# Converting w_out in two halves of one tile, nearer the front of batch 3, in an attention and two-layer kernel on one core

## The chip, the cores and the metric

The kernel runs on one core of one Trainium2 chip. The metric is device time of one execution in microseconds (us). All durations below come from one profiled execution of the kernel before, or from the times of its three runs.

## The reference, cut to what matters

```python
def reference(...):
    attn_out = _attn_ref(q, k, v)                 # 4 batches, 8 heads, 576 positions, masked softmax
    x = attn_out.transpose(0, 2, 1, 3).reshape(2304, 512)
    a = x @ w1;  b = x @ w2                       # 512 -> 1024
    x = (a * b @ w3) @ w_out                      # moe_w_out: 1024 -> 512
    h = x @ w_in                                  # moe2_w_in: 512 -> 2048
    g = h * (1.0 / (1.0 + np.exp(-1.702 * h)))
    return g @ w_out                              # moe2_w_out: 2048 -> 512
```

The weights arrive in 64-bit floats. The change is about the last factor, `moe2_w_out`, called w_out below.

## The kernel before

**Number formats.** Every matmul operand is split into a high and a low part (`split_hi` at L171 on ScalarE, `split_lo` at L177 on VectorE), and each product is three matmuls (`ORDER`: high times low, low times high, high times high). The 64-bit weights come in as tiles `raw` of 128 x 1024 pairs and are made into 32-bit floats by `to_f32`: two passes on ScalarE (L192 writes the tile `x` from `raw`, L193 scales the low words of `raw` in place) and three on VectorE (L194, L195, L196, all on `x`).

**Stages.** The first 466 us hold attention and the first layer, in four batches of 576 rows; batch 3 is the last of them and runs without attention work beside it. A batch is two halves of 288 columns; each half has eight groups m of two products (L354, 12 matmuls each; ScalarE copies the first to `abf` at L377, VectorE multiplies the second into it at L379, and L171 and L177 split the result into `ab`), and then four output groups n (L400, 24 matmuls over the eight `ab`), each copied to `ysb` by ScalarE (L406) and written to DRAM. All these products go through the four buffers of the PSUM pool `mm`.

Then comes the second layer, in three batches of 768 rows, each with eight quads (function `quad`). A quad has seven products of six matmuls (L666; the operands are `yq` and the split first factor `hl`), called its parts, and the adds and gelu of them on VectorE and ScalarE. After the fourth part of quad i and at its end stand the two output groups of quad i - 1 (`o_group`, L712, nine matmuls each, with the split w_out of that quad, `wt`, called w in the trace). The parts go through the four `mm` buffers too: the fifth part of a quad takes the buffer of the first, so it waits for the ScalarE copy of the first (L684, to the tile `c`).

**What is prepared in batch 3.** `weave` merges lists of functions by the marks between 0 and 1 that they carry; it sets the program order, and a scheduler at build time sets the order on each engine from that, each engine then running strictly in its order. Into batch 3 are woven: the split of the second layer's activations (`y_prep`), the first factor's fetch and split (`w_load(0)`, from the DRAM tensor `widram`), and the eight units of w_out (`u_conv`, units 8 to 15, marks 0.14 to 0.84 less one step). A unit is loaded into `raw` (1024 KB; two buffers, one in each of the pools `cv_a` and `cv_b`, unit i + 2 taking the buffer of unit i), converted in the one buffer `x` of `cv_a`, and written to the DRAM tensor `wodram` (L555, 512 KB). The next unit cannot write `x` before that transfer has landed.

**The join.** After batch 3 the pools of batch 3 and `cv_b` are closed, and the pool `p2`, which holds `c`, `u`, `sg` and the odd first factors, is laid over them. So the first `c` (L684) waits for the last readers of all that: the writes of `ysb` and the conversion of the last unit's `raw`. `wt_load(i)` brings one unit back from `wodram` (L643, into the one `raw` buffer of `cv_a`) and splits it into `wt[i]`; `w_load(n)` brings first factor n from `widram` (L617, into the one `x` buffer) and splits it into `hl`. Between the batches of the first layer and quad 0 the program has `wt_load(0)` and `w_load(1)`, and quad i of the first batch begins with `wt_load(i + 1)`.

All DMAs are issued by SyncE (SP), in its program order, on one queue.

Of the kernel before, what the change touches and what calls it, by code (L numbers as in the profile page):

```python
# [11 lines left out]
F32 = mybir.dt.float32  # L12
F32R = mybir.dt.float32r
# [8 lines left out]
P = 128  # L22
# [22 lines left out]
CW2 = 1024  # L45
# [3 lines left out]
NB = NT // BT  # L49
NU = 8  # L50
# [87 lines left out]
def body(ctx: ExitStack, tc, qk, vv, mask, w1, w2, w3t, wo, win, wout, out):  # L138
# [30 lines left out]
    def split_hi(hi, src, eng="act"):  # L169
        if eng == "act":  # L170
            nc.scalar.activation(hi, src, AF.Copy)  # L171
        else:
            nc.vector.tensor_copy(hi, src)

    def split_lo(lo, src, hi, eng="dve"):
        e = nc.vector if eng == "dve" else nc.gpsimd
        e.tensor_tensor(lo, src, r(hi), op=ALU.subtract)  # L177
# [352 lines left out]
    cv = None  # L530
    todo = {}
# [8 lines left out]

    def u_conv(i, last=False):
        raw = todo.pop(i)
        x = cv[0].tile([P, 2 * CW2], F32, tag="x", name="x")
        to_f32(x[:, :CW2], raw, CW2)
        if not last:
            u_load(i + 2)
        if i < NU:
            a21, a11, a12, a22, s1, s2, s3, s4 = (x[:, n * 256:(n + 1) * 256] for n in range(8))
            nc.vector.tensor_tensor(s1, a21, a22, op=ALU.add)
            nc.vector.tensor_tensor(s2, s1, a11, op=ALU.subtract)  # L550
            nc.vector.tensor_tensor(s3, a11, a21, op=ALU.subtract)
            nc.vector.tensor_tensor(s4, a12, s2, op=ALU.subtract)
            nc.sync.dma_start(widram[i], x[:, 256:])
        else:
            nc.sync.dma_start(wodram[i - NU], x[:, :CW2])  # L555

    def u_convs(lo, hi, ahead=True):
        return [lambda i=i: u_conv(i, not ahead and i + 2 >= hi) for i in range(lo, hi)]

    cvs = ExitStack()  # L560
    cv = [pool("cv", stack=cvs)]
# [24 lines left out]
    cv_a = pool("cva", stack=right1, side="right")  # L586
    cv_b = pool("cvb", stack=right2, side="right")
    cv = [cv_a, cv_b]
# [21 lines left out]

    wq = {}

    def w_load(n):
        if n < NB * NU:
            t = (p2 if n % 2 else cv_a).tile([P, 2, 7 * 256], F32R, tag="hl", name="hl")
            x = cv_a.tile([P, 2 * CW2], F32, tag="x", name="x")[:, 256:]
            nc.sync.dma_start(x, widram[n % NU])  # L617
            split_hi(t[:, 0], x)
            split_lo(t[:, 1], x, t[:, 0])
            wq[n] = t  # L620

    g = batch_groups(3)
    weave(
        g, [(0.02 + 0.06 * kk, lambda kk=kk: y_prep(0, kk)) for kk in range(2)] + [(0.09, lambda: w_load(0))]
        + [(0.1, lambda: u_load(NU)), (0.11, lambda: u_load(NU + 1))]
        + [(0.14 + 0.7 * i / NU, f) for i, f in enumerate(u_convs(NU, 2 * NU))],
    )
    p1s.close()
    right2.close()
# [8 lines left out]
    gl, gr = {}, {}  # L638
    acc_l, acc_r = {}, {}

    def wt_load(i):
        t = cv_a.tile([P, CW2], I64, tag="raw", name="raw").bitcast(F32)[:, :CW2]
        nc.sync.dma_start(t, wodram[i])  # L643
        w = wt[i].rearrange("p a c n -> p a (c n)")
        split_hi(w[:, 0], t)
        split_lo(w[:, 1], t, w[:, 0])

    def g_split(src):
        t = ring[used[0] % len(ring)]
# [24 lines left out]
    def quad(b, i, mid):  # L674

        w = wq.pop(b * NU + i)
        def part(f, b):
            ps = mm.tile([P, HT], F32, tag="mm", name="ps")
            product(ps, w, f, b)
            return ps  # L680

        p = part(0, 0)
        s1 = f32("c", 3)
        nc.scalar.activation(s1, p, AF.Copy)  # L684
        u2 = f32("u2", 2)
        add(u2, part(4, 4), s1)
        u3 = f32("u3", 2)
        add(u3, part(5, 5), u2)
        p = part(3, 3)
        c22 = f32("c", 3)  # L690
        add(c22, p, u3)
        add(u2, p, u2)
        mid()
        c11 = f32("c", 3)
        add(c11, part(1, 1), s1)
        right = [f32("gr", 16) for _ in range(2)]
        gelu(right[1], c22)
        gelu(c11, c11)
        gl[i] = g_split(c11)
        add(u3, part(2, 6), u3)  # L700
        gelu(u3, u3)
        gl[NU + i] = g_split(u3)
        add(u2, part(6, 2), u2)
        w_load(b * NU + i + 2)
        gelu(right[0], u2)
        gr[i], gr[NU + i] = right
# [18 lines left out]
                nc.scalar.activation(ob, acc[t], AF.Copy)  # L725
            nc.sync.dma_start(out[c0 + t * P:c0 + (t + 1) * P, :], ob)

    wt_load(0)
    w_load(1)
    for b in range(NB):  # L730
        left = [accp.tile([P, 512], F32, tag="acc", name="acc") for _ in range(HT // P)]
        for i in range(NU):
            if b == 0 and i + 1 < NU:
                wt_load(i + 1)
            quad(b, i, (lambda i=i: o_group(left, gl.pop(i - 1), i - 1, 0)) if i else (lambda: None))
            if i:
                o_group(left, gl.pop(NU + i - 1), i - 1, 1)
        for h in range(2):
            o_group(left, gl.pop(h * NU + NU - 1), NU - 1, h)
        put(left, b * BT)  # L740
        if b + 1 < NB:
            for kk in range(2):
                y_prep(b + 1, kk)
        right = [mm.tile([P, 512], F32, tag="mm", name="acc") for _ in range(HT // P)]
        for i in range(NU):
            for h in range(2):
                o_group(right, g_split(gr.pop(h * NU + i)), i, h)
        put(right, b * BT + HT)
# [35 lines left out]
```

## Time and profile before

| | us |
|---|---|
| three runs | 876.34, 878.00, 879.31; median 878.0 |
| profiled execution | 878.23 |
| its span, first to last instruction | 876.4 |
| PE (TensorE matmul) busy in the span | 833.2 |
| VectorE (DVE) busy | 587.2 |
| ScalarE (ACT) busy | 437.9 |

The profiled execution lies 0.2 us above the median, and 1.8 us of it lie outside the span. Two matmuls that follow each other overlap in the trace, so a duration of one is longer than the distance from one start to the next; where a rate is wanted, starts are subtracted. The trace's views used are: the page's slices, the timeline (instructions in order of time, with the idle time before a group and what ended it), and the windows (busy time, granted TensorE clock as a share of 2.4 GHz, DMA share and rate by stretch).

### The profile page before, as it was taken

Reading aid. Unit: us, or ns where it says so; the run is one execution under the profiler, and the core shown is the slowest. Engines: PE = TensorE matmul, PEld = TensorE weight load, DVE = VectorE, ACT = ScalarE, POOL = GpSimd, SP = SyncE. Lnnn points to the kernel's source line nnn. Section 1 sums busy time; section 2 is a strip of 40 time slices with the busy share of each in tenths; the row PEclk is TensorE's granted clock in tenths of the full one; section 3 lists DMA queues with packets and bytes.
Section 4 is the critical chain, followed back from the end, with each engine's and each line's share of the span. In section 5 each row is a group of like instructions: output and inputs, shape, how many; then the busy total and the mean of one; then the engine's idle time right before and its main releaser. Section 6 shows DMA issues by size and latency. Waiting matters only on the chain.

```text
span 876.4 us, 14097 instructions
## 1 busy us (share of the span) xinstructions
PE 833.2 (95%) x5288; PEld 744.0 (85%) x5288; DVE 587.2 (67%) x1369; ACT 437.9 (50%) x996; POOL 1.4 (0%) x8
## 2 busy tenths in 40 slices
PE   6999999999999999999993399999999999999998
PEld 3589899987889999999993389988999988999986
DVE  5999882368767778656342688876487765677740
ACT  6998762257565464444332455554244543434430
POOL 0000000000000000000000000000000000000000
PEclk9999999999999999999997699999999999999999
DMA  7765551244577553133445445213222232222010
GB/s 258 245 218 174 167 188 58 68 145 156 200 248 231 190 189 117 56 141 127 138 148 164 162 141 188 86 43 109 82 95 73 81 106 87 79 84 85 1 37 36
DMA packets 41700, 114.03 MB, mean 130 GB/s; under 512 B 4512, under 2 KB 25888, under 8 KB 38048
## 3 DMA queue, kind: packets, MB, share of 16 engines
q1 hardware_dynamic: 41632, 113.13, 37.9%
q8 instruction: 41, 0.67, 0.3%
q14 instruction: 27, 0.22, 0.1%
HBM read 88.60 MB, written 24.51 MB: 129 GB/s over the span
## 4 chain that ended last, share of the span: by engine, by line
PE 75%; DMA 9%; DVE 7%; ACT 7%; issue 1%; SPq 0%; ACTq 0%; DVEq 0%
PE acc L712 22%; PE ps L666 19%; PE ps L354 18%; PE ps L400 8%; DMA wodram<-x 4%; PE acc L469 2%; PE sc L250 2%; PE pv L308 2%; ACT sm L260 2%; DMA raw<-in_wout 1%; DMA x<-widram 1%; PE spare L498 1%; DVE x L196 1%; DVE x L195 1%; PE pt L286 1%
## 5 line engine op out<-in xcount | busy, mean ns | idle before, releaser
L666 PE MATMUL ps<-yq,hl 128*128 128x384 f32 x1008 | 188.9, 342 | 27.6 <-ACT c L684 21.7
L666 PEld LDWEIGHTS ps<-yq,hl 128*128 128x128 f32 x1008 | 181.3, 191 | 32.9 <-ACT c L684 22.2
L712 PE MATMUL acc<-w,w 128*128 128x512 f32 x864 | 205.2, 391 | 1.2 <-ACT w L171 1.2
L712 PEld LDWEIGHTS acc<-w,w 128*128 128x128 f32 x864 | 161.3, 188 | 34.4 <-ACT w L171 2.2
L400 PE MATMUL ps<-ab,w 128*128 128x288 f32 x768 | 108.1, 298 | 1.3 <-DVE ab L177 1.3
L400 PEld LDWEIGHTS ps<-ab,w 128*128 128x128 f32 x768 | 102.5, 188 | 4.6 <-DVE ab L177 2.4
L354 PE MATMUL ps<-xbh,w 128*128 128x288 f32 x512 | 103.4, 295 | 0.0
L354 PE MATMUL ps<-xah,w 128*128 128x288 f32 x512 | 102.1, 295 | 0.0
L354 PEld LDWEIGHTS ps<-xbh,w 128*128 128x128 f32 x512 | 82.2, 188 | 0.1
L354 PEld LDWEIGHTS ps<-xah,w 128*128 128x128 f32 x512 | 81.9, 188 | 0.0
L354 PE MATMUL ps<-xbl,w 128*128 128x288 f32 x256 | 79.6, 311 | 0.0
L354 PE MATMUL ps<-xal,w 128*128 128x288 f32 x256 | 76.4, 299 | 0.9 <-ACT abf L377 0.8
L657 ACT ACTIVATE sg<-c 128x384 f32<-128x384 f32 x48 | 25.1, 525 | 103.7 <-DVE c L672 103.5
L260 ACT ACTIVATE sm<-sm,st 96x128 f32<-96x128 f32 (+2 forms) x176 | 67.7, 388 | 17.7 <-DVE st L255 17.6
L193 ACT ACTIVATE raw<-raw 128x1024 int32<-128x1024 uint32 (+1 forms) x44 | 42.7, 972 | 48.3 <-DMA raw<-in_wout 32.2
L672 DVE TENSOR_TENSOR u<-ps,u 128x384 f32<-128x384 f32 x96 | 53.2, 554 | 11.2 <-PE ps L666 9.1
L177 DVE TENSOR_TENSOR hl<-x,hl 128x1792 fp32r<-128x1792 f32 x24 | 48.6, 2024 | 16.4 <-ACT hl L171 16.4
L379 DVE TENSOR_TENSOR abf<-ps,abf 128x288 f32<-128x288 f32 x64 | 28.9, 451 | 37.8 <-PE ps L354 31.6
L354 PEld LDWEIGHTS ps<-xbl,w 128*128 128x128 f32 x256 | 48.0, 188 | 3.8 <-issue 0.3
L171 ACT ACTIVATE ab<-abf 128x288 fp32r<-128x288 f32 x64 | 27.6, 442 | 46.4 <-DVE abf L379 39.0
L255 DVE CUSTOM_DVE_ANT_0 sm<-sc,msk 96x128 f32<-96x128 f32 (+2 forms) x176 | 40.9, 276 | 13.9 <-PE sc L250 8.4
L354 PEld LDWEIGHTS ps<-xal,w 128*128 128x128 f32 x256 | 48.0, 187 | 2.3 <-ACT abf L377 1.0
(82 smaller groups left out, 1061.2 us busy)
## 6 DMA issues: line engine op xcount, KB each, us to landing
x<-widram SPq DMA_DIRECT2D x24, 896.0 KB
raw<-in_w3t SPq DMA_DIRECT2D x17, 512.0 KB
raw<-in_w SPq DMA_DIRECT2D x8, 1024.0 KB
raw<-in_win SPq DMA_DIRECT2D x8, 1024.0 KB
raw<-in_wout SPq DMA_DIRECT2D x8, 1024.0 KB
widram<-x SPq DMA_DIRECT2D x8, 896.0 KB
qk<-in_qk SPq DMA_DIRECT2D x24, 224.0 KB
ydram<-ysb SPq DMA_DIRECT2D x32, 144.0 KB
```

Of the source, the lines that this page charges most:

```text
L171: nc.scalar.activation(hi, src, AF.Copy)
L177: e.tensor_tensor(lo, src, r(hi), op=ALU.subtract)
L193: nc.scalar.activation(ri[:, :, 0], ru[:, :, 0], AF.Copy, scale=LOW)
L255: nc.vector.tensor_tensor_reduce(sm[:nq, h, :nk], sc[:nq, h // 2, h % 2 * P:h % 2 * P + nk], msk[:nq, mi, :nk], -SCALE, 3e38, op0=ALU.add, ...
L260: nc.scalar.activation(sm[:nq, h, :nk], sm[:nq, h, :nk], AF.Exp, bias=st[:nq, 0, h:h + 1], scale=-1.0, accum_out=st[:nq, 1, h:h + 1],)
L354: nc.tensor.matmul(ps, ws[a][m // 2][:, at:at + P], xh[c][:, k, cols], start=(k == 0 and (a, c) == ORDER[0]), stop=(k == KC - 1 and (a, c) ...
L379: nc.vector.tensor_tensor(f, ps, f, op=ALU.mult)
L400: nc.tensor.matmul(st[0], wfs[a][k][:, n * P:(n + 1) * P], hold[hb, k][:, c], start=(k == 0 and (a, c) == ORDER[0]), stop=(k == MC - 1 and ...
L657: nc.scalar.activation(sg, src, AF.Sigmoid, scale=1.702)
L666: nc.tensor.matmul(ps, w[:, a, f * 256 + kk * P:f * 256 + (kk + 1) * P], yq[:, b, kk, c], start=(kk == 0 and (a, c) == ORDER[0]), stop=(kk ...
L672: nc.vector.tensor_tensor(dst, x, y, op=ALU.add)
L712: nc.tensor.matmul(acc[t], g[:, a, t * P:(t + 1) * P], wt[i][:, c, half], start=(i == half == 0 and (a, c) == ORDER[0]), stop=(i == NU - 1 ...
```

## The change

Three edits. The units of w_out are converted in two halves of one `x` tile in turn: the tile is allocated once, at unit 8, and unit i uses columns 0 to 1023 or 1024 to 2047. Their marks go from 0.14 + 0.7 i / 8 to 0.12 + 0.6 i / 8. And fetch and split of a factor become functions of their own: ahead of quad 0 only the fetches of first factor 1 and of w_out unit 0 are left, and their splits, with the whole `wt_load(1)`, stand in quad 0 where its middle function is called, behind the fourth part. `wt_load(i + 1)` of quads 1 to 6 stays as it is.

```diff
     def u_conv(i, last=False):
         raw = todo.pop(i)
-        x = cv[0].tile([P, 2 * CW2], F32, tag="x", name="x")
+        if i < NU:
+            x = cv[0].tile([P, 2 * CW2], F32, tag="x", name="x")
+        else:
+            if i == NU:
+                todo["x"] = cv[0].tile([P, 2 * CW2], F32, tag="x", name="x")
+            x = todo["x"][:, i % 2 * CW2:(i % 2 + 1) * CW2]
...
-    def w_load(n):
+    def w_fetch(n):
         if n < NB * NU:
-            t = (p2 if n % 2 else cv_a).tile([P, 2, 7 * 256], F32R, tag="hl", name="hl")
             x = cv_a.tile([P, 2 * CW2], F32, tag="x", name="x")[:, 256:]
             nc.sync.dma_start(x, widram[n % NU])
+            wq[n] = x
+
+    def w_split(n):
+        if n < NB * NU:
+            x = wq[n]
+            t = (p2 if n % 2 else cv_a).tile([P, 2, 7 * 256], F32R, tag="hl", name="hl")
             split_hi(t[:, 0], x)
             split_lo(t[:, 1], x, t[:, 0])
             wq[n] = t
...
-        + [(0.14 + 0.7 * i / NU, f) for i, f in enumerate(u_convs(NU, 2 * NU))],
+        + [(0.12 + 0.6 * i / NU, f) for i, f in enumerate(u_convs(NU, 2 * NU))],
...
-    wt_load(0)
-    w_load(1)
+    w_fetch(1)
+    first_wt = wt_fetch(0)
+
+    def mid_first():
+        w_split(1)
+        wt_split(0, first_wt)
+        wt_load(1)
+
...
-            if b == 0 and i + 1 < NU:
+            if b == 0 and 0 < i < NU - 1:
                 wt_load(i + 1)
-            quad(b, i, (lambda i=i: o_group(left, gl.pop(i - 1), i - 1, 0)) if i else (lambda: None))
+            quad(b, i, (lambda i=i: o_group(left, gl.pop(i - 1), i - 1, 0)) if i else mid_first if b == 0 else (lambda: None))
```

What that makes of the order on two engines is shown at three places; a name in brackets is a semaphore that the instruction waits for (DMAHW with a number: the landing of one DMA). Line numbers of the changed kernel are its own: its L686, L704, L732 and L621 are L666, L684, L712 and L617 of before.

First, ScalarE in the first half of batch 3, from the first unit's L192 (the second L193 and L192 of before belong to units 10 and 9). Before:

```order
L192 ACTIVATE x<-raw 128x1024 [waits DVE_49]
L171 ACTIVATE ab<-abf 128x288 [waits DVE_49]
L377 ACTIVATE abf<-ps 128x288 [waits PE_49]
L171 ACTIVATE ab<-abf 128x288 [waits DVE_49]
L406 ACTIVATE ysb<-ps 128x288 [waits DMAHW6_49,PE_49]
L193 ACTIVATE raw<-raw 128x1024 [waits DMAHW3_49,Activation_49]
L406 ACTIVATE ysb<-ps 128x288 [waits DMAHW7_49,PE_49]
L192 ACTIVATE x<-raw 128x1024 [waits DMAHW4_49]
```

The same place now:

```order
L192 ACTIVATE x<-raw 128x1024 [waits DVE_49]
L192 ACTIVATE x<-raw 128x1024
L171 ACTIVATE ab<-abf 128x288 [waits DVE_49]
L377 ACTIVATE abf<-ps 128x288 [waits PE_49]
L171 ACTIVATE ab<-abf 128x288 [waits DVE_49]
L406 ACTIVATE ysb<-ps 128x288 [waits DMAHW6_49,PE_49]
L193 ACTIVATE raw<-raw 128x1024 [waits DMAHW3_49,Activation_49]
L406 ACTIVATE ysb<-ps 128x288 [waits DMAHW7_49,PE_49]
L192 ACTIVATE x<-raw 128x1024 [waits DMAHW4_49]
L193 ACTIVATE raw<-raw 128x1024 [waits DMAHW5_49,Activation_49]
L192 ACTIVATE x<-raw 128x1024 [waits DMAHW6_49]
```

The L192 of units 8 and 9 now stand side by side, the second without a wait, and those of units 10 and 11 follow ahead of the third and fourth `ysb`; DMAHW3 to DMAHW6 are there the load of unit 10, the write of unit 8, the load of unit 11 and the write of unit 9, so unit 10 waits for unit 8's write alone and unit 11 for unit 9's.

Second, ScalarE at the end of batch 3, up to the first part's copy to `c`. Before (three units, 13 to 15, with their L193 and L192):

```order
L406 ACTIVATE ysb<-ps 128x288 [waits DMAHW7_49,PE_49,Activation_49]
L193 ACTIVATE raw<-raw 128x1024 [waits DMAHW0_49,DVE_49]
L192 ACTIVATE x<-raw 128x1024 [waits DMAHW1_49]
L406 ACTIVATE ysb<-ps 128x288 [waits DMAHW2_49,PE_49,Activation_49]
L193 ACTIVATE raw<-raw 128x1024 [waits DMAHW5_49,DVE_49,Activation_49]
L192 ACTIVATE x<-raw 128x1024 [waits DMAHW6_49]
L192 ACTIVATE x<-raw 128x1024 [waits DMAHW7_49,DVE_49]
L171 ACTIVATE w_66<-raw 128x1024 [waits DMAHW0_49]
L684 ACTIVATE c<-ps 128x384 [waits DMAHW3_49,DVE_49,DMAHW4_49,PE_49,Activation_49]
```

The same place now:

```order
L192 ACTIVATE x<-raw 128x1024 [waits DMAHW2_49]
L171 ACTIVATE ab<-abf 128x288 [waits DVE_49]
L377 ACTIVATE abf<-ps 128x288 [waits PE_49,Activation_49]
L171 ACTIVATE w_66<-raw 128x1024 [waits DMAHW4_49]
L171 ACTIVATE ab<-abf 128x288 [waits DVE_49]
L406 ACTIVATE ysb<-ps 128x288 [waits DMAHW3_49,PE_49]
L171 ACTIVATE w_68<-raw 128x1024 [waits DMAHW6_49]
L406 ACTIVATE ysb<-ps 128x288 [waits PE_49]
L406 ACTIVATE ysb<-ps 128x288 [waits DMAHW7_49,PE_49,Activation_49]
L171 ACTIVATE w_70<-raw 128x1024 [waits DMAHW2_49]
L406 ACTIVATE ysb<-ps 128x288 [waits DMAHW1_49,PE_49,Activation_49]
L704 ACTIVATE c<-ps 128x384 [waits DMAHW3_49,DVE_49,DMAHW4_49,PE_49,Activation_49]
```

The last unit's L192 is now ahead of the last two `ab` of batch 3 (groups m = 6 and 7 of its second half), and the high splits of w_out units 0, 1 and 2 (w_66, w_68, w_70) stand among the last `ab` and `ysb`; no conversion is left between the last `ysb` and `c`.

Third, VectorE at the same place, up to the first add of quad 0. Before:

```order
L194 TENSOR_SCALAR x<-x 128x1024 [waits DMAHW7_49,Activation_49]
L195 SCALAR_TENSOR_TENSOR x<-raw,x 128x1024 [waits DMAHW5_49,DVE_49]
L177 TENSOR_TENSOR w_66<-raw,w_66 128x1024 [waits DMAHW0_49,Activation_49]
L196 ISA x<-raw,x 128x2048 [waits DVE_49]
L672 TENSOR_TENSOR u_5580<-ps,c 128x384 [waits DMAHW3_49,DMAHW2_49,DMAHW4_49,PE_49,Activation_49]
```

The same place now:

```order
L194 TENSOR_SCALAR x<-x 128x1024 [waits Activation_49]
L177 TENSOR_TENSOR ab<-abf,ab 128x288 [waits Activation_49]
L195 SCALAR_TENSOR_TENSOR x<-raw,x 128x1024 [waits DMAHW1_49,DVE_49]
L196 ISA x<-raw,x 128x2048 [waits DVE_49]
L379 TENSOR_TENSOR abf<-ps,abf 128x288 [waits PE_49,Activation_49]
L177 TENSOR_TENSOR w_66<-raw,w_66 128x1024 [waits DMAHW4_49,Activation_49]
L177 TENSOR_TENSOR ab<-abf,ab 128x288 [waits Activation_49]
L177 TENSOR_TENSOR w_68<-raw,w_68 128x1024 [waits DMAHW6_49,Activation_49]
L177 TENSOR_TENSOR w_70<-raw,w_70 128x1024 [waits DMAHW2_49,Activation_49]
L692 TENSOR_TENSOR u_5564<-ps,c 128x384 [waits DMAHW3_49,DMAHW1_49,DMAHW4_49,DMAHW0_49,DMAHW7_49,PE_49,Activation_49]
```

The last multiply and the last low split of batch 3 (L379 and the second L177 of `ab`) now stand behind the last unit's three passes and behind the low split of w_out unit 0, which itself waits for a transfer from `wodram`.

## Rows read from the trace of the kernel before

**Rows 1.** The page's busy time by engine, and TensorE in 40 slices.

```profile
PE 833.2 (95%) x5288; PEld 744.0 (85%) x5288; DVE 587.2 (67%) x1369; ACT 437.9 (50%) x996; POOL 1.4 (0%) x8
...
PE   6999999999999999999993399999999999999998
```

**Rows 2.** Timeline of TensorE over the join: start, us, group; in brackets idle before.

```profile
450.34 12.85 PE L400 MATMUL ps<-ab,w 128*128 128x288 f32 x96
463.03 3.29 PE L666 MATMUL ps<-yq,hl 128*128 128x384 f32 x18
470.67 1.89 PE L666 MATMUL ps<-yq,hl 128*128 128x384 f32 x6 [4.35 <-ACT ysb L406]
494.23 5.33 PE L666 MATMUL ps<-yq,hl 128*128 128x384 f32 x18 [21.66 <-ACT c L684]
500.75 3.64 PE L712 MATMUL acc<-w,w 128*128 128x512 f32 x14 [1.20 <-ACT w L171]
...
513.31 0.79 PE L666 MATMUL ps<-yq,hl 128*128 128x384 f32 x3 [0.28 <-ACT hl L171]
515.37 5.48 PE L666 MATMUL ps<-yq,hl 128*128 128x384 f32 x21 [1.27 <-DVE hl L177]
520.68 2.25 PE L712 MATMUL acc<-w,w 128*128 128x512 f32 x9
522.77 3.31 PE L666 MATMUL ps<-yq,hl 128*128 128x384 f32 x18
525.92 2.25 PE L712 MATMUL acc<-w,w 128*128 128x512 f32 x9
```

**Rows 3.** Timeline of ScalarE, 400 to 500 us: conversions and the join.

```profile
407.20 1.14 ACT L192 ACTIVATE x<-raw 128x1024 f32<-128x1024 f32 x1 [0.52 <-DVE hl L177]
...
419.76 1.11 ACT L192 ACTIVATE x<-raw 128x1024 f32<-128x1024 f32 x1
...
468.00 1.14 ACT L193 ACTIVATE raw<-raw 128x1024 int32<-128x1024 uint32 x1 [7.33 <-DMA raw<-in_wout]
469.20 1.12 ACT L192 ACTIVATE x<-raw 128x1024 f32<-128x1024 f32 x1
...
488.14 1.12 ACT L192 ACTIVATE x<-raw 128x1024 f32<-128x1024 f32 x1 [6.26 <-DMA wodram<-x]
...
493.68 0.49 ACT L684 ACTIVATE c<-ps 128x384 f32<-128x384 f32 x1 [3.06 <-DVE x L196]
```

**Rows 4.** Timeline of VectorE: unit 8's three passes, an L379, a low split of w_out.

```profile
408.37 0.69 DVE L194 TENSOR_SCALAR x<-x 128x1024 int32<-128x1024 int32 x1
...
409.35 1.22 DVE L195 SCALAR_TENSOR_TENSOR x<-raw,x 128x1024 int32<-128x1024 int32 x1
410.60 1.22 DVE L196 CUSTOM_DVE_ANT_0 x<-raw,x 128x2048 uint16<-128x2048 uint16 x1
411.74 0.45 DVE L379 TENSOR_TENSOR abf<-ps,abf 128x288 f32<-128x288 f32 x1
...
491.17 1.22 DVE L177 TENSOR_TENSOR w<-raw,w 128x1024 fp32r<-128x1024 f32 x1
```

**Rows 5.** Timeline of SP: issue of unit 10's load and of unit 8's write.

```profile
411.90 0.33 SPq L538 DMA_DIRECT2D raw<-in_wout  x1
412.28 0.42 SPq L555 DMA_DIRECT2D wodram<-x  x1
```

**Rows 6.** Windows: PE, PEld, DVE, ACT, POOL busy; granted clock, DMA share, GB/s.

```profile
425.00:430.00 5.00, 5.00 (x39) 5.00 (x38) 0.46 (x1) 0.41 (x1) 0.00 (x0) 1.00 0.90 261
470.00:475.00 5.00, 1.89 (x6) 1.38 (x6) 3.14 (x3) 0.62 (x2) 0.00 (x0) 0.62 0.23 43
515.00:520.00 5.00, 4.63 (x18) 4.63 (x19) 4.47 (x9) 2.16 (x6) 0.00 (x0) 0.66 0.50 184
528.00:870.00 342.00, 342.00 (x1700) 307.81 (x1699) 231.10 (x380) 143.88 (x240) 0.00 (x0) 1.00 0.22 77
```

**Rows 7.** The chain that ended last: start, us, what; one fetch of a first factor.

```profile
497.43 4.79 DMA x<-widram
```

More of the change, by code (lines that the diff above doesn't have):

```diff
@@ L620, in w_load @@
             wq[n] = t
+    def w_load(n):
+        w_fetch(n)
+        w_split(n)
     g = batch_groups(3)
@@ L639, in body, with wt_fetch, wt_split @@
     acc_l, acc_r = {}, {}
-    def wt_load(i):
+    def wt_fetch(i):
         t = cv_a.tile([P, CW2], I64, tag="raw", name="raw").bitcast(F32)[:, :CW2]
         nc.sync.dma_start(t, wodram[i])
+        return t
+    def wt_split(i, t):
         w = wt[i].rearrange("p a c n -> p a (c n)")
@@ L646, in wt_load @@
         split_lo(w[:, 1], t, w[:, 0])
+    def wt_load(i):
+        wt_split(i, wt_fetch(i))
     def g_split(src):
```

## The prediction

> **What bounds the kernel now.** Read the slices first: TensorE is busy 95% of the span, and the one hole behind the start is two slices of 3 tenths in the middle [rows 1]. Next the timeline of TensorE over that hole [rows 2]. It shows two long waits: 4.35 us for the last `ysb` copy, 21.66 us for the copy of quad 0's first part to `c`; then short ones (1.20, 0.28, 1.27). Everything from 528 to 870 is 342.00 us busy of 342 [rows 6]: there only matmuls count, so what is won at the join is won at the end, and nothing behind it can be won.
>
> How much is there to win? A rate is a difference of starts: 18 L666 in 525.92 - 522.77 = 3.15, so 0.175 each; 9 L712 in 2.09, so 0.232; 96 L400 in 12.69, so 0.132 [rows 2]. The first three parts of quad 0 end at 463.03 + 18 x 0.175 = 466.2. From there to 520.68 stand 90 L666 (the other 66 of the 84 of quads 0 and 1, and 24 of quad 2) and 18 L712: 15.75 + 4.18 = 19.9. The stretch takes 54.5, so **34.6 us** are lost: 26.0 in the two long waits, 2.75 in the short ones, the rest at half clock (granted 0.62 and 0.66 in two windows, between the levels of 1.2 and 2.4 GHz [rows 6]; 18 matmuls took 5.3 instead of 3.15 [rows 2]).
>
> Who ends the long waits? ScalarE [rows 3]. The L192 of the eight units come one by one: the first at 407.20, the sixth at 469.20, five steps of 12.4. A step is 1.1 on ScalarE, the three VectorE passes (3.1 with nothing between [rows 4]), and then the landing of the transfers: the write issued at 412.28 [rows 5] lets unit 9's L192 run at 419.76, at most 7.5 later. Eight steps do not fit into batch 3. Unit 14's L193, waiting 7.33 for its load, stands ahead of the last `ysb`; the last unit's L192 runs at 488.14, and only behind its last pass may `c` be written, 493.68 [rows 3]. VectorE and ScalarE are far from full; the bound is the one `x` buffer.
>
> **Two halves.** No instruction is added or removed but a few waits; order and dependences change. In the built order unit 10 waits for unit 8's write and unit 11 for unit 9's, so two chains run beside each other. Unit 8's L192 stays at 407.20, unit 9's follows at 408.3. VectorE now has both units in a row, and one `ab` among them: 408.4 + 2 x 3.1 + 0.4 = 415.0, where unit 8 alone ended at 411.8 [rows 4]. The last two `ab` of this half come some 4 us later for that; their matmuls are late in the order (18 of L400's first 24 need neither, and 15 of the next group's were pulled ahead), so I take 0.4 for it.
>
> Each unit moves 1.05 MB in and 0.52 MB out. Unit 11's load and unit 9's write, issued at 415.0, come behind unit 8's pair: alone they would land at 415.4 + 7.5 = 422.9; 3.15 MB from 412.2 on at the 261 GB/s of the busy window [rows 6] need 12.1, so 424.6 with half a us to start. I take 424.6, as two pairs are in flight for certain. From there the second chain makes two more steps (units 13, 15). One lasts 12.4 if the transfers do not meet, and 3.45 MB (two pairs, two `ysb`) / 261 GB/s = 13.2 if they queue; I take 13.2. So **unit 15's L192 runs at 424.6 + 2 x 13.2 = 451.0** (ends: 422.9 + 24.8 = 447.7, and 453.8 with 14 a step and a unit 11 at 425.8).
>
> **What is late next.** Not `c`: all conversions are ahead of it now. But ScalarE has the last two `ab` of batch 3 behind unit 15's L192, and VectorE has the last one behind unit 15's passes and w_out unit 0's low split. From 451.0: L192 1.1, passes 3.1, one `ab` 0.45, L379 0.45, that low split 1.2, the last `ab` 0.45 [rows 3, 4]: **457.8**. TensorE starts L400 of the second half as before at about 450.3, can do 27 matmuls (0.132 each) and stands at 453.9. It waits **3.9**. Then 69 are left, 9.1: batch 3 ends at 466.9 instead of 463.03. The `raw` fetch of w_out unit 0 must have landed by about 455 for this, with unit 14 converted some 1.5 ahead of unit 15; it does so narrowly.
>
> **Quads 0 and 1** then need 84 L666 and 18 L712, 14.7 + 4.2 = 18.9, if nothing waits. The last `ysb` stands behind w_out unit 2's high split on ScalarE, but its buffer is wanted only by the fourth part, 3 us later; `c` needs the write of that `ysb`, and the fifth part needs `c` 4 us after the first. First factor 1: its fetch starts when unit 15's write has landed (about 459), takes 4.8 [rows 7], and its split starts behind `c`, about 470 to 474; quad 1's first matmul comes at 474, so I add 0.2. On SP the fetches of w_out units 1 and 2 now stand among the `ysb` writes and hold them while they wait for VectorE's low splits; that is 1 to 2 us each against a cover of 3. If that cover fails it costs up to 2. Quad 2 begins at 466.9 + 19.1 = 486.0, before at 513.31: **27.3**. Its own first 24 matmuls took 520.68 - 513.31 = 7.4 instead of 4.2 [rows 2]; first factor 2 is now there in time (split by 482), so **3.2** more.
>
> **The clock.** The new wait of 3.9 in batch 3 is not free behind it. A wait of 1.27 was followed by 21 matmuls in 5.31 instead of 3.68 [rows 2], at a granted clock of 0.66 over the window [rows 6]. I charge the new one the same **1.6**; the bounds are nothing, and 2.2, what 18 matmuls lost behind the longest wait [rows 2].
>
> A rule of the Trainium skill speaks against this change here: "TensorE: Matmul & The Clock Gate", section "Why this matters for your kernels", says to leave no idle gaps between bursts of matmuls, since one idle spell puts the array back to its half clock. The change puts such a gap into a batch that has none now; by the rule the charge falls, and without it the sum would be 1.6 better. The row with 1.27 of idle agrees with it [rows 2, 6].
>
> **Sum**, against the profiled execution's 878.2 (the median of the runs, 878.0, lies 0.2 below): 27.3 + 3.2 - 1.6 = 28.9, so **849.3**.
>
> **Rivals.**
> (a) The transfers are the bound: more than 261 GB/s is not granted with loads and writes mixed, and each landing is held by the next pair, so that a step takes 16 instead of 13.2 and unit 15 comes at about 458. ScalarE is strictly in order, so batch 3 waits us for us: 7 worse, some 856. For it: the busy window has a DMA share of 0.90 at 261 GB/s, and two chains ask for nearly all of that. Against it: the load and write of one unit landed within 7.5 in all steps.
> (b) The transfers do not queue: unit 15 at 447.7, the wait in batch 3 shrinks to 0.6 and no half clock follows: 27.3 + 3.3 + 3.2 = 33.8, 844.4. For it: a window's mean of 261 contains starts of transfers. All 34.6 gone would be 843.6.
> (c) Slower: the halves do not part, because a unit's first pass waits for the landing of both writes to the tile. Then unit 10 comes at 424.6 and unit 15 five steps of 12.4 later, 486.6; but now the last `ab` of batch 3 stand behind it on ScalarE: 486.6 + 6.8 + 9.1 + 19.1 puts quad 2 at 521.6, 8.3 later than now, less the 3.2, and 2.2 at half clock: 885.5. It decides in that direction as soon as unit 15's L192 is later than 451.0 + 28.9 = 480. Against it: the brackets in the order name one landing each.
> (d) Nothing gained: the chain is slowed to between 477 and 483. I see no mechanism that stops there.
>
> **How the numbers follow.** About 0.3% (2.6 us) is what a measurement of this kernel can tell from no change. My forecast, 846 to 853.5, has 0.66; (a), 853.5 to 862, 0.20; (b) 0.08; (c) 0.04; (d) 0.02. Range: 844.5 to 857 leaves out the far part of (a), (c), (d) and the lowest part of (b), about 0.2 together. Faster 0.94, same 0.02, slower 0.04.
>
> **What the profile after would show.** Right: L192 in pairs about 1 us apart at first, the last near 451; no wait of TensorE for `c`; one new wait inside L400 of the second half, 3 to 5 us, ended by VectorE's `ab`; slices of 9 where the 3s were; quad 2 near 486. If L400's wait is over 8, it is (a); if there is none, (b); if `ab` waits until 490, (c). The prediction is wrong also if quads 0 to 2 wait for `hl` or for the last `ysb` by more than 2, or if L354 of batch 3's second half is held by ScalarE's loads, which I take as covered by the four `mm` buffers.

## The result, and the profile after

The changed kernel takes **849.3 us** (median of 4 runs, 846.7 to 851.4), beside 877.2 of the kernel before on the same chip: ratio **0.968**, 95% interval 0.964 to 0.972. The forecast was 849.3. Two later sets gave 848.6 (0.966, interval 0.964 to 0.967) and 850.0 (0.968, 0.964 to 0.971). One execution of e11 and one of e15 below (1005.4 and 1342.3 us) ran at a mean granted clock of 0.76 and 0.56 and are left out of their ratios.

The page after, TensorE's busy time, the 40 slices and the granted clock:

```profile
PE 830.1 (98%) x5288; PEld 741.9 (87%) x5288; DVE 586.4 (69%) x1369; ACT 436.3 (51%) x996; POOL 1.4 (0%) x8
...
PE   6999999999999999999998999999999999999998
...
PEclk9999999999999999999999999999999999999999
```

The two slices of 3 [rows 1] are 8 and 9. The work is the same, 5288 matmuls; the share rises from 95% to 98% because the span shrinks.

Where to start measuring? The profiled execution took 851.4 and was the slowest of its four. It is behind already where the change has done nothing yet: of the 20 us from 40 on TensorE was busy 18.20 at a granted clock of 0.91, while another execution of the same kernel (e0 below) had 19.79 at 1.00. So I count from a point ahead of the change, the start of the last 60 L400 of batch 2, and compare executions by their distance from it. First before, then after (timeline of TensorE: start, us, group):

```profile
376.74 8.21 PE L400 MATMUL ps<-ab,w 128*128 128x288 f32 x60
```

```profile
380.03 8.21 PE L400 MATMUL ps<-ab,w 128*128 128x288 f32 x60
...
453.35 3.84 PE L400 MATMUL ps<-ab,w 128*128 128x288 f32 x27
460.06 9.38 PE L400 MATMUL ps<-ab,w 128*128 128x288 f32 x69 [2.87 <-DVE ab L177]
469.28 4.33 PE L686 MATMUL ps<-yq,hl 128*128 128x384 f32 x24
473.88 3.56 PE L686 MATMUL ps<-yq,hl 128*128 128x384 f32 x19 [0.27 <-ACT c L704]
478.19 4.33 PE L686 MATMUL ps<-yq,hl 128*128 128x384 f32 x23 [0.75 <-DVE hl L177]
...
489.69 4.33 PE L686 MATMUL ps<-yq,hl 128*128 128x384 f32 x24
493.85 2.25 PE L732 MATMUL acc<-w,w 128*128 128x512 f32 x9
```

After runs 3.29 late at that point (380.03 - 376.74). The waits of 4.35 and 21.66 [rows 2] are gone; the one wait foreseen inside L400 has come, 2.87, ended by VectorE's `ab`. From the point to quad 2's first matmul it is 489.69 - 380.03 = **109.7**, before 513.31 - 376.74 = **136.6**. I call that stretch the join.

ScalarE after; the rows that answer to [rows 3] are the L192, one for each unit:

```profile
410.50 2.20 ACT L192 ACTIVATE x<-raw 128x1024 f32<-128x1024 f32 x2 [0.52 <-DVE hl L177]
...
426.41 1.16 ACT L192 ACTIVATE x<-raw 128x1024 f32<-128x1024 f32 x1
...
453.18 1.13 ACT L192 ACTIVATE x<-raw 128x1024 f32<-128x1024 f32 x1
...
470.12 1.06 ACT L171 ACTIVATE w<-raw 128x1024 fp32r<-128x1024 f32 x1 [3.35 <-DMA raw<-wodram]
471.09 0.39 ACT L406 ACTIVATE ysb<-ps 128x288 f32<-128x288 f32 x1
473.33 0.49 ACT L704 ACTIVATE c<-ps 128x384 f32<-128x384 f32 x1 [1.86 <-DMA ydram<-ysb]
```

Units 8 and 9 stand back to back (x2), and the last unit comes at 453.18 - 3.29 = 449.9 on the axis of before, 38 us ahead of its 488.14 [rows 3]. The last three rows are the next chain: w_out unit 2's split waits for its fetch, the last `ysb` stands behind it, `c` waits for that `ysb`'s write.

The VectorE rows that decide the new wait: unit 15's last passes, the last L379, w_out unit 0's low split, and only then the last `ab`:

```profile
455.32 1.22 DVE L195 SCALAR_TENSOR_TENSOR x<-raw,x 128x1024 int32<-128x1024 int32 x1
456.57 1.23 DVE L196 CUSTOM_DVE_ANT_0 x<-raw,x 128x2048 uint16<-128x2048 uint16 x1
457.71 0.45 DVE L379 TENSOR_TENSOR abf<-ps,abf 128x288 f32<-128x288 f32 x1
458.41 1.23 DVE L177 TENSOR_TENSOR w<-raw,w 128x1024 fp32r<-128x1024 f32 x1 [0.25 <-ACT w L171]
459.55 0.45 DVE L177 TENSOR_TENSOR ab<-abf,ab 128x288 fp32r<-128x288 f32 x1
```

### The profile page after: what moved, and what is told of

The parts are those of the page before. It is cut to its first block, busy times and chain, and to the rows that moved or that the text cites. A ratio compares the mean times of both kernels' runs of the same rounds, so it can differ in the third digit from the quotient of the medians.

```text
span 849.7 us, 14089 instructions
## 1 busy us (share of the span) xinstructions
PE 830.1 (98%) x5288; PEld 741.9 (87%) x5288; DVE 586.4 (69%) x1369; ACT 436.3 (51%) x996; POOL 1.4 (0%) x8
## 4 chain that ended last, share of the span: by engine, by line
PE 81%; DMA 8%; ACT 6%; DVE 4%; issue 1%; SPq 0%; ACTq 0%; DVEq 0%
PE acc L732 23%; PE ps L686 20%; PE ps L354 19%; PE ps L400 8%; PE acc L469 6%; PE sc L250 2%; DMA wodram<-x 2%; PE pv L308 2%; ACT sm L260 2%; DMA raw<-in_w 1%; DMA abf<-abdram 1%; ACT raw L193 1%; PE pt L286 1%; DMA raw<-in_wout 1%; DMA raw<-in_wo 1%
## 5 line engine op out<-in xcount | busy, mean ns | idle before, releaser
L732 PE MATMUL acc<-w,w 128*128 128x512 f32 x864 | 204.9, 391 | 0.0
L732 PEld LDWEIGHTS acc<-w,w 128*128 128x128 f32 x864 | 161.4, 188 | 32.7 <-ACT w L171 0.7
L686 PE MATMUL ps<-yq,hl 128*128 128x384 f32 x1008 | 184.1, 337 | 1.0 <-DVE hl L177 0.8
L686 PEld LDWEIGHTS ps<-yq,hl 128*128 128x128 f32 x1008 | 177.6, 188 | 5.1 <-DVE hl L177 1.1
L400 PE MATMUL ps<-ab,w 128*128 128x288 f32 x768 | 108.3, 298 | 4.8 <-DVE ab L177 4.8
L400 PEld LDWEIGHTS ps<-ab,w 128*128 128x128 f32 x768 | 102.5, 188 | 8.3 <-DVE ab L177 6.2
L354 PE MATMUL ps<-xbh,w 128*128 128x288 f32 x512 | 104.2, 296 | 0.0
L354 PE MATMUL ps<-xah,w 128*128 128x288 f32 x512 | 102.0, 294 | 0.0
L354 PEld LDWEIGHTS ps<-xbh,w 128*128 128x128 f32 x512 | 82.9, 189 | 0.1
L354 PEld LDWEIGHTS ps<-xah,w 128*128 128x128 f32 x512 | 81.9, 188 | 0.0
L354 PE MATMUL ps<-xbl,w 128*128 128x288 f32 x256 | 80.1, 313 | 0.0
L354 PE MATMUL ps<-xal,w 128*128 128x288 f32 x256 | 76.3, 298 | 0.1
L177 DVE TENSOR_TENSOR hl<-x,hl 128x1792 fp32r<-128x1792 f32 x24 | 48.6, 2023 | 13.8 <-ACT hl L171 13.8
L193 ACT ACTIVATE raw<-raw 128x1024 int32<-128x1024 uint32 (+1 forms) x44 | 42.8, 974 | 27.5 <-DMA raw<-in_wout 10.6
L379 DVE TENSOR_TENSOR abf<-ps,abf 128x288 f32<-128x288 f32 x64 | 28.9, 452 | 36.0 <-PE ps L354 31.1
L354 PEld LDWEIGHTS ps<-xbl,w 128*128 128x128 f32 x256 | 48.5, 189 | 3.9 <-issue 0.6
L354 PEld LDWEIGHTS ps<-xal,w 128*128 128x128 f32 x256 | 48.0, 187 | 1.3 <-DVE abf L379 0.4
```

Source lines behind the costliest of these rows:

```text
L193: nc.scalar.activation(ri[:, :, 0], ru[:, :, 0], AF.Copy, scale=LOW)
L354: nc.tensor.matmul(ps, ws[a][m // 2][:, at:at + P], xh[c][:, k, cols], start=(k == 0 and (a, c) == ORDER[0]), stop=(k == KC - 1 and (a, c) ...
L379: nc.vector.tensor_tensor(f, ps, f, op=ALU.mult)
L400: nc.tensor.matmul(st[0], wfs[a][k][:, n * P:(n + 1) * P], hold[hb, k][:, c], start=(k == 0 and (a, c) == ORDER[0]), stop=(k == MC - 1 and ...
L686: nc.tensor.matmul(ps, w[:, a, f * 256 + kk * P:f * 256 + (kk + 1) * P], yq[:, b, kk, c], start=(kk == 0 and (a, c) == ORDER[0]), stop=(kk ...
L732: nc.tensor.matmul(acc[t], g[:, a, t * P:(t + 1) * P], wt[i][:, c, half], start=(i == half == 0 and (a, c) == ORDER[0]), stop=(i == NU - 1 ...
```

## The experiments

Theory: the two halves are the whole gain; what is left is the wait inside L400, made by late work ahead of the last `ab`, with half clock behind it. Rivals: the split behind `c` is what frees quad 0; the transfers are the bound. Unless it says otherwise, an edit is against the changed kernel.

**Which part of the change acts: e4, e10, e1.** e4 leaves the halves out and keeps the rest; its rows on ScalarE, VectorE and SyncE stand in the order of before, one for one. e10 lets the halves overlap by one column, so that neither is free of the other. e1 has the halves alone, with the marks and the splits of before.

```
e4:
-        if i < NU:
...
-            x = todo["x"][:, i % 2 * CW2:(i % 2 + 1) * CW2]
+        x = cv[0].tile([P, 2 * CW2], F32, tag="x", name="x")
e10:
-            x = todo["x"][:, i % 2 * CW2:(i % 2 + 1) * CW2]
+            x = todo["x"][:, i % 2 * (CW2 - 1):i % 2 * (CW2 - 1) + CW2]
e1 (against the kernel before):
-        x = cv[0].tile([P, 2 * CW2], F32, tag="x", name="x")
+        if i < NU:
...
+            x = todo["x"][:, i % 2 * CW2:(i % 2 + 1) * CW2]
```

> The other two parts of the change alone: the conversions' places in batch 3 and the split of first factor 1 behind c, with one x buffer for each unit as before. Theory (these two move nothing as long as the conversions come one by one): 877 to 879 us, no difference from before. Rival (the split placed behind c frees c by itself): c is copied 2 to 5 us earlier, 873 to 876 us.

> The changed kernel, but the second half begins one column ahead of the first one's end, so that each unit has to wait for the one before it, as if there were one buffer. Theory (the independence of the halves is the whole gain, and ScalarE and VectorE keep an order that puts late units behind the ab): the time of the kernel before, 876 to 880 us, with L192 every 12.4 us again. Rival (c) of the prediction, units that stay ahead of the ab in the order though they come late: 885 us. Rival (the marks or the split behind c help by themselves): 870 us or less.

> Only the two halves; first factor 1 is split where it was before, ahead of quad 0's copy to c. Theory (the halves are the whole gain, the placement behind c is worth a little): no wait of 21 us for c, c comes 1.7 to 3 us later than in the changed kernel for one high split and one more conversion ahead of it, 851 to 853 us, 0.971 of before. Rival (placing the split behind c is what frees quad 0): TensorE waits for c by 10 us or more, 860 us or above.

Measured: e4 **878.7** (ratio 1.001, 0.999 to 1.003), e10 **877.5** (1.000, 0.998 to 1.001), e1 **851.8** (0.970, 0.968 to 0.972). Without independent halves `c` comes as late as ever; TensorE of e10:

```profile
494.26 5.72 PE L686 MATMUL ps<-yq,hl 128*128 128x384 f32 x18 [21.21 <-ACT c L704]
...
515.21 3.91 PE L686 MATMUL ps<-yq,hl 128*128 128x384 f32 x21 [1.27 <-DVE hl L177]
```

So the halves carry the gain. In e10 too the rows of the three engines stand in the order of before; whether the halves act by the write that is no longer waited for, or by the order that the scheduler can build from it, these runs do not part.

The marks and the split behind `c` are worth nothing alone (e4), and with the halves about 3 us: e1's 851.8 stands beside 848.6 of the changed kernel in the same set. Up to the last `ysb` e1's rows stand in the changed kernel's order, so it is the split and not the marks. The join takes 114.6 in e1's profiled execution (854.9, the slowest of its four) instead of 109.7 to 110.7. In it `c` comes 16.0 behind the end of the wait in L400 (459.72), after 13.3 (473.33 - 460.06). Some 1.1 of that is half clock, which lasted longer here: the 69 L400 behind the wait took 11.9, in e0 below 10.8. The rest is the split: first factor 1's high split stands ahead of `c` on ScalarE, and its low split on VectorE ahead of quad 0's adds, for which TensorE then waits:

```profile
474.12 1.70 ACT L171 ACTIVATE hl<-x 128x1792 fp32r<-128x1792 f32 x1 [1.86 <-DMA ydram<-ysb]
475.73 0.47 ACT L689 ACTIVATE c<-ps 128x384 f32<-128x384 f32 x1
```

```profile
478.40 1.31 PE L671 MATMUL ps<-yq,hl 128*128 128x384 f32 x6 [0.82 <-DVE u L677]
```

**The changed kernel again: e0, e14.** No edit.

> The changed kernel itself, beside which the other three of this set are read. 846.7 to 851.4 us by its earlier executions. If half clock really does not follow the wait of 2.87 us inside L400 of batch 3's second half, every window from 425 to 525 us shows a granted clock near 1.0 again, and quad 2's first 24 L666 take 4.2 us; if that was luck of one execution, one window shows 0.6 to 0.9 and the time is 1.6 to 2.2 us longer.

> The changed kernel once more, beside which the two others of this set are read: 847 to 851 us, with the wait of 2.9 us inside L400 of batch 3's second half. From the start of the last 60 L400 of batch 2 to quad 2's first matmul 109.5 to 111 us, with or without half clock behind the wait, if the half clock lies under the chain to first factor 1; 112 us or more with half clock if it does not.

The profiled executions took 848.4 and 848.5. TensorE of e0, and two windows of it (PE, PEld, DVE, ACT, POOL busy; granted clock, DMA share, GB/s):

```profile
375.88 8.21 PE L400 MATMUL ps<-ab,w 128*128 128x288 f32 x60
...
450.19 3.83 PE L400 MATMUL ps<-ab,w 128*128 128x288 f32 x27
456.97 10.93 PE L400 MATMUL ps<-ab,w 128*128 128x288 f32 x69 [2.95 <-DVE ab L177]
467.74 11.71 PE L686 MATMUL ps<-yq,hl 128*128 128x384 f32 x66
...
486.60 4.33 PE L686 MATMUL ps<-yq,hl 128*128 128x384 f32 x24
490.77 2.25 PE L732 MATMUL acc<-w,w 128*128 128x512 f32 x9
```

```profile
455.00:460.00 5.00, 3.03 (x12) 3.04 (x13) 1.60 (x3) 1.03 (x3) 0.00 (x0) 0.70 0.69 239
460.00:465.00 5.00, 5.00 (x38) 5.00 (x38) 1.23 (x1) 1.66 (x3) 0.00 (x0) 0.96 0.91 291
```

The wait is the same, but half clock follows: the 69 L400 take 467.74 - 456.97 = 10.8, after 469.28 - 460.06 = 9.2. Yet from the end of the wait to quad 2 both take 29.63 (486.60 - 456.97 and 489.69 - 460.06), and e14 29.61. What the slow L400 lose, quads 0 and 1 do not wait: 18.9 there, 20.4 after; `c` comes 13.3 behind the end of the wait in all three executions. So e0's expectation was wrong in its second half: half clock came, and no longer time with it. The join is 110.7 in e0 and e14, and 109.7 after.

**The transfers: e7.** Each unit is written a second time, to a place that nothing reads.

```
             nc.sync.dma_start(wodram[i - NU], x[:, :CW2])
+            nc.sync.dma_start(wo2dram[i - NU], x[:, :CW2])
```

> The changed kernel, but each converted unit of w_out is also written to a second place in DRAM that nothing reads: 0.52 MB more for each unit, 1.05 MB more for a step of both chains. Theory (a step is the time from a write's issue to its landing and two dependent passes, not the rate): steps of 12.3 to 15 stay within 1 us, the last L192 moves by 3 us at the most, the time by 0 to 3 us. Rival (the transfers are the bound at some 261 GB/s): 1.05 MB more are 4 us a step, the last L192 moves by 8 to 12 us and the wait inside L400 with it, 8 us slower or more.

Measured **854.4** (0.974, 0.971 to 0.976). ScalarE of e7 (its lines are one higher), units 8 and 9, then 11, 13 and 15:

```profile
408.30 2.18 ACT L193 ACTIVATE x<-raw 128x1024 f32<-128x1024 f32 x2 [0.52 <-DVE hl L178]
...
428.13 1.14 ACT L193 ACTIVATE x<-raw 128x1024 f32<-128x1024 f32 x1 [0.90 <-DMA wo2dram<-x]
...
444.45 1.13 ACT L193 ACTIVATE x<-raw 128x1024 f32<-128x1024 f32 x1 [0.79 <-DMA wo2dram<-x]
...
459.57 1.14 ACT L193 ACTIVATE x<-raw 128x1024 f32<-128x1024 f32 x1 [1.12 <-DMA wo2dram<-x]
```

The same of e0, units 11 and 13:

```profile
422.35 1.15 ACT L192 ACTIVATE x<-raw 128x1024 f32<-128x1024 f32 x1
...
434.95 1.16 ACT L192 ACTIVATE x<-raw 128x1024 f32<-128x1024 f32 x1
```

From unit 8 to unit 15 it is 51.3 in e7 and 43.7 in e0 (from 406.35 to 450.04), 7.6 more. Counted from unit 8, unit 11 is 3.8 later than in e0, unit 13 is 7.6 later, and unit 15 no more than that: two steps grew by 3.8 and 3.7, the third by nothing, since in e0 something else than the transfers sets it (an order on ScalarE, shown in the next section). In the two, 1.05 MB cost what some 280 GB/s give, an estimate from these rows. That is the 4 us a step of the rival, not the 1 of the theory: the transfers do set a step. The time grew by some 5 (854.4, beside 848.6 to 850.0 of the changed kernel), not by the rival's 8. The wait in L400 did not grow, it was 0.95: this kernel's built order has unit 15 behind the last `ab`, and the loss went to `c` and first factor 1 instead.

**The wait inside L400: e8, e9, e11.** e8 gives w_out unit 0's low split to GpSimd, e9 lets the chains start earlier and puts first factor 0 behind them, e11 exchanges the two `raw` buffers, which puts that whole split behind the last `ab`.

```
e8:
-        split_lo(w[:, 1], t, w[:, 0])
+        split_lo(w[:, 1], t, w[:, 0], "pool" if i < 1 else "dve")
e9:
-        ... + [(0.09, lambda: w_load(0))]
+        ... + [(0.85, lambda: w_load(0))]
e11:
-        raw = cv[i % len(cv)].tile(...)
+        raw = cv[(i + (i >= NU)) % len(cv)].tile(...)
```

> The changed kernel, with the low split of w_out unit 0 on GpSimd instead of VectorE; the last ab of batch 3 then stands right behind the last L379 on VectorE. Theory (the wait of 2.87 us inside L400 ends with a chain on VectorE of which that split is 1.23): the wait shrinks to about 1.4, the time by 1.0 to 1.5 us, and quad 0's first L712 does not wait. Rival 1 (the wait is set by the last conversion's passes and the last L379 alone): wait and time unchanged. Rival 2 (GpSimd is slow with it or holds VectorE's port): w_out unit 0 is ready late, an L712 waits for it, 2 us or more lost.

> The changed kernel, with the fetch and split of first factor 0 written at 0.85 of batch 3 instead of 0.09, so that the x buffer goes to the conversions earlier and the two chains start some 8 us sooner. Theory (the wait inside L400 is the distance of the last conversion from the front of batch 3): the last L192 runs at 441 to 445 us from the span's start, the wait of 2.87 is gone or under 0.5, 2 to 3 us faster than the changed kernel, about 846.5. Rival (what is late is passed on): first factor 0 is now ready too late and quad 0's first L666 waits for hl by 2 us or more, no gain, or slower.

> The changed kernel, with the two raw buffers of batch 3 exchanged, so that the odd units (9, 11, 13, 15) stand in the one that the fetch of w_out unit 0 takes over. That fetch then waits for unit 15's passes and not for unit 14's, and in the built order the split of w_out unit 0 stands behind the last ab of batch 3 on ScalarE and VectorE, and w_out unit 2's behind quad 0's c. Theory (that one split is what is left of the wait inside L400, and the w_out splits hold the last ysb and c): the wait of 2.9 us shrinks to about 2.0, quads 0 and 1 take 18.9 us or less behind L400 at full clock, 846 to 847.5 us, 1 to 2 faster than the changed kernel in the same set of runs. Rival (w_out comes too late for the first L732, or first factor 1 is still what quad 1 waits for): the wait shrinks and quads 0 and 1 take so much longer, no change.

e8 took **854.0** (0.971, 0.969 to 0.972). The last `ab` did start at once, but took 2.37 instead of 0.45, ending 0.3 behind GpSimd's split; the wait grew to 5.06. Of that 0.8 is the order of TensorE, which changed with it: 21 L400 stood ahead of the wait instead of 27. GpSimd, VectorE and TensorE of e8:

```profile
458.68 2.34 POOL L177 TENSOR_TENSOR w<-raw,w 128x1024 fp32r<-128x1024 f32 x1 [456.70 <-ACT w L171]
458.97 2.37 DVE L177 TENSOR_TENSOR ab<-abf,ab 128x288 fp32r<-128x288 f32 x1 [0.85 <-ACT ab L171]
...
461.39 3.97 PE L400 MATMUL ps<-ab,w 128*128 128x288 f32 x15 [5.06 <-DVE ab L177]
```

The Trainium skill states this in "SBUF — State Buffer", section "SBUF: two separate sides": VectorE with two inputs in SBUF and GpSimd take one pair of ports for a whole instruction, and the other waits. The rows agree (2.37 beside 2.34).

e9 took **853.4** (0.971, 0.969 to 0.973). The last L192 did come at 441.16. But first factor 0's low split now stood ahead of the last `ab` on VectorE, and the wait was 3.06, as long as ever:

```profile
456.67 2.02 DVE L177 TENSOR_TENSOR hl<-x,hl 128x1792 fp32r<-128x1792 f32 x1 [2.95 <-ACT hl L171]
458.61 0.45 DVE L177 TENSOR_TENSOR ab<-abf,ab 128x288 fp32r<-128x288 f32 x1
```

e11 took **850.2** (0.969, 0.967 to 0.971), no gain. The last `ab` was ready 5.95 behind unit 15's L192 (451.99 to 457.94) instead of 6.9 (e0), as expected; but the wait did not shrink to the 2.0 expected: the order of TensorE changed here too, and only 21 L400 stood ahead of the wait instead of 27:

```profile
452.15 3.03 PE L400 MATMUL ps<-ab,w 128*128 128x288 f32 x21
457.99 11.71 PE L400 MATMUL ps<-ab,w 128*128 128x288 f32 x75 [2.81 <-DVE ab L177]
```

The six that went behind it, 0.8, are about what the earlier `ab` had gained. So the cause of the wait shows (e8's `ab` and wait grew together, e11's `ab` came earlier), but none of the three made the wait shorter (5.06, 3.06, 2.81), and none is faster. What the kernel would gain without the wait is left to the next three.

**Without the wait: e12, e13, e15.** e12 fetches first factor 0 into a `raw` buffer at the front of batch 3, so that the chains start early and no factor comes late. e13, and e15 which is the same kernel again, also put w_out unit 3 where its split can't stand ahead of `c`.

```
e12:
-            x = cv_a.tile([P, 2 * CW2], F32, tag="x", name="x")[:, 256:]
+            if n:
+                x = cv_a.tile([P, 2 * CW2], F32, tag="x", name="x")[:, 256:]
+            else:
+                x = cv_b.tile([P, CW2], I64, tag="raw", name="raw").bitcast(F32)[:, 256:]
...
-        ... + [(0.09, lambda: w_load(0))]
+        ... + [(0.02, lambda: w_load(0))]
e13, e15, beside that:
-    for n, i in enumerate((0, 2, 4, 6, 1, 3, 5, 7)):
+    for n, i in enumerate((0, 2, 4, 8, 1, 3, 5, 7)):
...
-    ring = [slot[8 + i // 2][...
+    ring = [slot[(6, 9, 10, 11)[i // 2]][...
...
-        t = ring[used[0] % len(ring)]
+        t = ring[used[0] % len(ring)] if used[0] else lead
```

Here `lead` is the half of slot 8 that the first split of a second product's input takes, and w_out unit 3 waits for its readers.

> The changed kernel, with first factor 0 fetched into a raw buffer at the very front of batch 3 and not into x. The x buffer then goes to the conversions some 8 us sooner without making first factor 0 late, and in the built order no split stands ahead of the last ab but w_out unit 0's high one, which lands well before. Theory (the wait inside L400 needs a late conversion or split ahead of the last ab): no wait of more than 0.5 us in L400's second half and no half clock behind it. But w_out unit 3's high split now stands ahead of c on ScalarE, and the w_out fetches come some 6.5 us apart: c at 472 to 475 us, TensorE waits for it by 3 to 6 us, and the time is within 2 us of the changed kernel's. Rival (the last ab is late for another reason): a wait over 2 us stays in L400, and c's comes on top, 3 us slower or more.

> The kernel with first factor 0 in a raw buffer, and w_out unit 3 put into a tensor that the first half of quad 1's second product still reads, so that its split can't stand ahead of c; the ring of the second product's inputs gives one place up for it. Theory: no wait in L400, c right behind the last ysb at about 468, TensorE waits for it by 0 to 2 us, 844 to 846.5 us, 2 to 4 us faster than the changed kernel. Rival (first factor 1, whose split stands behind c, is what quad 1 waits for anyway): quad 1 waits for hl by what L400 gained, no change.

> The kernel with first factor 0 in a raw buffer and w_out unit 3 behind c, a second time, on another set of runs. If its 2.3 us in the stretch from the last 60 L400 of batch 2 to quad 2 are real, that stretch is 108 to 109 us again, without half clock, and the time 845.5 to 848.5 us; if the stretch is 110 us or more, it is no better than the changed kernel.

e12 took 850.9 (0.968, 0.965 to 0.970), e13 **848.2** (0.964, 0.962 to 0.967), e15 849.0 (0.968, 0.965 to 0.971). e13 and e15 lie above what was expected of them (844 to 846.5, and 845.5 to 848.5). TensorE of e13:

```profile
375.93 8.21 PE L400 MATMUL ps<-ab,w 128*128 128x288 f32 x60
...
414.53 9.78 PE L400 MATMUL ps<-ab,w 128*128 128x288 f32 x72 [1.28 <-DVE ab L177]
...
450.43 12.74 PE L400 MATMUL ps<-ab,w 128*128 128x288 f32 x96
463.01 4.33 PE L690 MATMUL ps<-yq,hl 128*128 128x384 f32 x24
468.49 3.59 PE L690 MATMUL ps<-yq,hl 128*128 128x384 f32 x19 [1.15 <-ACT c L708]
472.80 4.33 PE L690 MATMUL ps<-yq,hl 128*128 128x384 f32 x23 [0.72 <-DVE hl L177]
...
484.27 4.33 PE L690 MATMUL ps<-yq,hl 128*128 128x384 f32 x24
```

All 96 L400 run through. Counted from the start of the join, batch 3 ends 4.7 earlier than in e14 (463.01 - 375.93 = 87.1; 467.77 - 375.95 = 91.8), but quad 2 begins only 2.3 earlier (108.3; 110.7): quads 0 and 1 take 21.3 instead of 18.9, now waiting for `c` and for first factor 1. No split stands ahead of `c` any more, but the write of the last `ysb` took 4.28 to land, where it took 1.86 after. e12 gave 109.2, with 1.26 for `c` where 3 to 6 had been expected, and 1.18 for first factor 1. e15 gave 109.3; in it the first half's wait was 2.08 and half clock followed. Is e13 a better kernel? Its times lie 1.8 below e14's in the same set, but the intervals overlap, so that stays open.

## Why the prediction was right

On the time axis of before, that is with 0.86 added to e0 and 3.29 taken from after:

| step | predicted | e0 | after |
|---|---|---|---|
| unit 11's L192 | 424.6 | 423.2 | 423.1 |
| unit 15's L192 | 451.0 | 450.9 | 449.9 |
| last `ab` ready | 457.8 | 457.8 | 456.7 |
| wait in L400 | 3.9 | 2.95 | 2.87 |
| half clock behind it | 1.6 | 1.6 | 0 |
| end of batch 3 | 466.9, with the clock 468.5 | 468.6 | 466.0 |
| quads 0 and 1 | 19.1 | 18.9 | 20.4 |
| quad 2, with the clock | 487.6 | 487.5 | 486.4 |
| quad 2's first 24 L666 | 4.2 | 4.2 | 4.2 |

The join and quad 2's own 24 give 25.85 + 3.2 = 29.1 in e0, 30.1 after; the sum was 28.9. The chain of reasons holds: two chains of units, `c` no longer late, one new wait in L400 with 27 matmuls ahead of it and 69 behind, none for `c` of any size. That the median meets the forecast to the tenth is luck: the four executions lie 4.7 apart, and details that were 1 to 2 us off, some too early and some too late, cancel. They are:

- **The sum added two terms that cover each other.** The charge of 1.6 for half clock was right where half clock came (two of three executions), and the 0.2 for quads 0 and 1 was right there too. At full clock the charge is 0, but the quads wait 1.5, for what the prediction named as a cover that could fail: the fetches of w_out hold the last `ysb`, hence `c` and first factor 1. Either way quad 2 begins 29.6 behind the wait. e13, without a wait in batch 3's second half, still waits for `c` and first factor 1. So the term to write was the larger of the two, about 1.6 with or without half clock; added up at their full sizes (1.6 and 1.5) they would have made the forecast 1.3 longer than it was.
- **The transfers' rate was taken a little low, and a window's rate is no ceiling.** 3.15 MB were to take 12.4, from 412.2 to 424.6 (the terms given add up to 424.8); in e0 it is 11.0, from 412.2 to 423.2, and unit 11 came 1.4 early. As the price of a step 261 GB/s was near: e7's two steps give some 280, and in e13 units 13 and 15 come 13.1 and 12.6 behind 11 and 13, where the prediction had 13.2. But 5 us of after show 410 GB/s, while in e7 a window at a share of 0.97 (450 to 455) moved 255. After:

```profile
445.00:450.00 5.00, 5.00 (x39) 5.00 (x38) 1.29 (x3) 2.79 (x4) 0.00 (x0) 1.00 0.99 410
```

- **The last step was an order, not a transfer.** The second chain's two steps were not 13.2 each but 12.6 and 15.1 (e0; 422.35, 434.95, 450.04), and the sum hid it. Unit 15's L193 ran at 448.67, right behind an `ab` that had waited 2.09 for VectorE's L379, with no wait for its load:

```profile
448.32 0.45 ACT L171 ACTIVATE ab<-abf 128x288 fp32r<-128x288 f32 x1 [2.09 <-DVE abf L379]
448.67 1.18 ACT L193 ACTIVATE raw<-raw 128x1024 int32<-128x1024 uint32 x1
```

- **The wait** was 1 too long on paper, and at 2.9 just under the 3 to 5 named. In e0 the last `ab` is where it was predicted, and TensorE is late: L400 of the second half starts at 451.05 on the axis of before, not at 450.3. Of that 0.6 was lost in the first half, for which the prediction took 0.4 and then left it out of the sum. L354 was held for 0.86 by ScalarE and VectorE (waits of 0.66 and 0.20), little more than the 0.76 of before. The late start costs nothing: it comes off the wait. In after TensorE is on time and the `ab` 1.1 early.
- **The rivals.** (a) fell because a step of the changed kernel did not take 16, though e7 shows that the transfers set it. (b) had the wait nearly gone, and it is not; where it is gone, in e13, the join and quad 2's own 24 give 28.2 + 3.2 = 31.4, not the 33.8 of (b), since `c` and first factor 1 are late next. (c) is not what overlapping halves give: in e10 the scheduler puts late units behind the `ab`, and the time is that of before.

## What to carry to other kernels

When a chain of fetch, convert and write is held by one buffer, look first at whether two of its items fit into that buffer side by side; here nothing else of the change had any effect without it. Behind a removed wait, list what is late next and take the larger of two costs that overlap, not their sum: taking 4.7 us out of batch 3 gave 2.3. An item moved out of the way of one engine's queue can change the order of another's, as e11's six matmuls did, so a local gain has to be read at the next common point.

## What the runs showed of the hardware

- Half clock behind a wait of TensorE is not the same from one execution to the next. Behind the wait of the changed kernel it came in two executions of three (2.95 and 3.15, not 2.87); inside L400 it also came behind 2.08 (e15), 2.81 (e11), 3.06 (e9), 3.21 (e1) and 5.06 (e8), and not behind 0.95 to 1.33 (e7, e12, e13, e9). Behind the 1.27 ahead of quad 2's 21 L666 it came in before (5.3 for them [rows 2]) but not in e10 (515.21 to 518.96, 3.75), nor in e4, whose rows stand in the order of before (516.81 to 520.56, 3.75). From 365 to 530 us the granted clock fell only behind idle gaps, as the section of the Trainium skill that the prediction weighed says ("TensorE: Matmul & The Clock Gate", "Why this matters for your kernels"). It did not fall behind each of them, as the prediction had it, so the row with 1.27, which the prediction read as agreeing, does not show the rule by itself.
- A subtraction of 0.45 on VectorE took 2.37 beside one of 2.34 on GpSimd (e8).
- Loads of 1 MB and writes of 0.5 MB, mixed, moved 410 GB/s over 5 us of after. A high DMA share is not a rate: in e7 windows of 5 us at shares of 0.97 to 1.02 moved 255, 384 and 422 GB/s (from 450, 455 and 420).
